# Splitting the last output projection of an attention + FFN kernel into early partial sums

## The chip, the cores and the metric

The kernel runs on one core of one Trainium2 chip. The metric is device time in microseconds (us) of one execution; lower is better. A span is the part of it that the profile shows, some 2 us shorter. Every run also lists its mean granted TensorE clock (1.0 is full speed). All runs quoted here are of the state "fast", the undisturbed one. In the views of the profile PE is TensorE, PEld its weight loads, DVE is VectorE, ACT ScalarE, POOL GpSimd and SP SyncE, which here only starts transfers; Lnnn is a line of the kernel.

## The reference

One transformer layer in parallel form: `x + attention(layernorm(x)) + ffn(layernorm(x))`, with 2048 tokens, width 640, 32 query heads of 20 channels that share one K and one V head, and a hidden layer of 1536 with squared ReLU. Data is bf16.

```python
# cut to what matters
q = (xn @ wq).reshape(B, S, 32, 20); k = xn @ wk; v = xn @ wv
p = softmax(q k^T * 20 ** -0.5)
attn = (p @ v).reshape(B, S, 640) @ wo      # the output projection
h = relu(xn @ w1 + b1) ** 2
out = x + attn + h @ w2 + b2
```

## The kernel before

Attention is done in 32 blocks: 4 chunks of 512 queries, and in each chunk 8 groups of 4 heads. A block has 16 steps of 128 keys, so there are 512 steps. In each step TensorE computes scores into PSUM banks 0 to 5, ScalarE exponentiates them (two instructions of 128x1024), and TensorE multiplies the result by V into bank 6 (the PV matmuls). Everything else (Q projection, FFN, normalisation, output projection) is cut into small pieces that a planner puts under the exponentials, one after the other through the one remaining bank, MISCB (7). Where a step has room, padding matmuls on zeros keep TensorE busy.

At the end of a block the accumulator is copied, transposed, divided by the softmax sum and transposed back into `OTn[:, chunk, group]`. The output projection of a chunk needs all 8 groups, so that of the last chunk can only start when every exponential is done:

```python
def op_pe(tt, ch, part=None):            # 128 tokens tt, half ch of the 640 columns
    gs = list(range(G)) if part is None else ...   # 8 head groups, in two parts of 4
    pairs = [(OTn[:, qc % 2, g, tl * 128:(tl + 1) * 128],
              wo_pad[:, g, ch * WOC:(ch + 1) * WOC]) for g in gs]
    ... mm_group(e, bank(MISCB, WOC), pairs, first, last)

def op_evac(tt, ch):                     # out_stage = PSUM + out_acc (fp32: x + FFN)
    ... e.tensor_tensor(out=out_stage[...], in0=bank(MISCB, WOC), in1=out_acc[...], op=ALU.add)

# [cut] the main loop over 512 steps, then:
pe_pv(NU - 1, 0)
fin_done_slot[NB - 1] = chain_fin(NB - 1, NU)      # last block's normalise/transpose
for tt in range(4 * (QC - 1), 4 * QC):             # the last chunk's 4 x 2 pieces
    for ch in range(2):
        op_pending.append((tt, ch, fin_done_slot[NB - 1] + 1))
```

## Time and profile before

| | before |
|---|---|
| time, median of the first 4 runs | 1014.39 us (1011.52 to 1017.11) |
| the profiled run | 1011.52 us, span 1009.8 us |
| ScalarE busy | 965.1 us, 96% of the span |
| last PV matmuls start | 988.95 us |
| the 8 projection pieces of the tail | 992.80 to 1007.51 us |

From the page of the profiled run of the kernel before: its span and the busy time of each engine.

```profile
span 1009.8 us, 16754 instructions
PE 821.8 (81%) x7425; PEld 297.7 (29%) x7483; DVE 212.5 (21%) x429; ACT 965.1 (96%) x1070; POOL 101.5 (10%) x138
```

ScalarE (ACT) sets the pace. The waits view says how much of its time the 1024 exponentials lost; columns are engine and line, what it waited for, total us, times, longest.

```profile
ACT PT L1092 <- PE ps L1076: 10.5, 12, 6.7
```

Only 10.5 us in the whole span, so work that lies under the exponentials is free as long as it does not hold them up. What is not free is the end. The chain of waits that ended last, in order of time (start, length, what), kernel before:

```profile
988.95 0.43 PE ps L1104 x4
...
992.32 0.43 DVE OTn L1169
992.75 0.05 issue
992.80 1.27 PE ps L462 x8
994.08 0.02 issue
994.10 0.50 DVE out_stage L1256
994.60 0.05 issue
994.65 1.27 PE ps L462 x8
...
1007.02 0.49 DVE out_stage L1256
```

TensorE multiplies 8 head groups (1.27 us), VectorE adds (0.50 us), TensorE waits for the bank and starts the next piece; the two steps from engine to engine, called hops here, take 0.02 and 0.05 us. That makes 1.84 us a round, eight rounds, 14.71 us. No engine is busy for more than part of it. Then the last store takes 2.3 us to the end of the span.

### The profile page before, as it was taken

The page shows a single profiled execution, that of the slowest core. Times are in us where ns is not written, and L with a number is a line of the kernel's source. Part 1 is how long each engine was busy: PE and PEld are TensorE (multiplying, and loading weights), DVE is VectorE, ACT ScalarE, POOL GpSimd, SP SyncE. Part 2 cuts the span into 40 slices and gives each one's busy share as a digit, 9 for nine tenths or more (in the row PEclk, how much of TensorE's full clock was granted, in tenths as well). Part 3 has the DMA queues.
Part 4 walks back from the last instruction along what each step waited for, and adds up shares of the span by engine and source line. Part 5 has one row for each costly group of instructions (what it writes and reads, how often), then busy time and mean ns, then how long its engine had stood idle before and what let it go on. Part 6 is the DMA issues. An engine that isn't in the chain of part 4 may idle for free.

```text
span 1009.8 us, 16754 instructions
## 1 busy us (share of the span) xinstructions
PE 821.8 (81%) x7425; PEld 297.7 (29%) x7483; DVE 212.5 (21%) x429; ACT 965.1 (96%) x1070; POOL 101.5 (10%) x138
## 2 busy tenths in 40 slices
PE   2878899878988887899888889987778877777775
PEld 2322244222432322244222224432222222222222
DVE  6522222222222222222222122210111111011102
ACT  6599999999999999999999999999999999999991
POOL 7021100121000012100120020000000000000000
PEclk9999999999999999999999999999999999999999
DMA  9100000000000000000000000000000000000000
GB/s 303 26 1 1 1 1 2 1 2 1 2 1 14 14 1 2 1 1 1 1 2 14 14 1 2 1 1 1 1 1 8 14 8 1 1 1 1 1 1 26
DMA packets 9433, 11.93 MB, mean 12 GB/s; under 512 B 1809, under 2 KB 8722, under 8 KB 9362
## 3 DMA queue, kind: packets, MB, share of 16 engines
q1 hardware_dynamic: 9362, 10.87, 3.3%
q8 instruction: 58, 0.95, 0.4%
q14 instruction: 13, 0.11, 0.0%
HBM read 8.25 MB, written 2.62 MB: 11 GB/s over the span
## 4 chain that ended last, share of the span: by engine, by line
ACT 89%; PE 7%; DVE 3%; issue 0%; DMA 0%; ACTq 0%; POOL 0%; SPq 0%; DVEq 0%
ACT PT L1092 88%; PE ps L462 2%; PE ps L1108 1%; PE ps L1076 1%; PE ps L1104 1%; DVE O_un L1135 1%; PE ps L1142 1%; ACT PT L632 1%; DVE out_stage L1256 1%; DVE r_tmp L908 1%; PE ps L722 0%; ACT PT L637 0%; PE ps L996 0%; DMA x_sb<-in_A_x_dram 0%; DVE xnT L737 0%
## 5 line engine op out<-in xcount | busy, mean ns | idle before, releaser
L1092 ACT ACTIVATE PT<-ps 128x1024 bf16<-128x1024 f32 x1024 | 940.1, 1237 | 10.5 <-PE ps L1076 10.5
L1076 PE MATMUL ps<-QT,KT_aug 21*128 21x512 bf16 x2048 | 202.4, 385 | 126.5 <-ACT PT L1092 121.0
L1108 PE MATMUL ps<-ones_bf,zeros_bf 128*32 128x512 bf16 x883 | 261.7, 380 | 0.0
L1104 PE MATMUL ps<-PT,V_aug 128*32 128x512 bf16 x2048 | 205.1, 390 | 8.0 <-DVE O_un L1135 7.3
L1076 PEld LDWEIGHTS ps<-QT,KT_aug 21*128 21x128 bf16 x2048 | 51.9, 91 | 320.9 <-ACT PT L1092 300.8
L1108 PEld LDWEIGHTS ps<-ones_bf,zeros_bf 128*32 128x32 bf16 x883 | 85.1, 96 | 53.9 <-issue 0.3
L954 POOL TENSOR_TENSOR Qsq<-QT 128x512 bf16<-128x512 bf16 x32 | 33.2, 1038 | 656.3 <-DVE QT L949 646.5
L1104 PEld LDWEIGHTS ps<-PT,V_aug 128*32 128x32 bf16 x2048 | 52.5, 93 | 125.5 <-issue 108.7
L462 PE MATMUL ps<-xnT,w_sb 128*128 128x512 bf16 x216 | 64.6, 383 | 4.2 <-issue 2.4
L915 POOL TENSOR_TENSOR h2T<-r_tmp 128x512 bf16<-128x512 bf16 x48 | 49.9, 1039 | 177.2 <-DVE r_tmp L908 177.2
L908 DVE TENSOR_SCALAR r_tmp<-ps,b_sb 128x512 bf16<-128x512 f32 x48 | 36.0, 751 | 136.1 <-PE ps L462 136.1
L462 PE MATMUL ps<-w_sb,h2T 128*128 128x160 bf16 x768 | 64.2, 233 | 0.0
L1135 DVE COPY O_un<-ps 128x512 f32<-128x512 f32 x32 | 22.0, 688 | 183.4 <-PE ps L1108 162.2
L462 PEld LDWEIGHTS ps<-w_sb,h2T 128*128 128x128 bf16 x768 | 51.6, 98 | 27.2 <-DVE out_acc L1216 21.7
L933 PE MATMUL ps<-xnT,wq_raw 128*20 128x512 bf16 x640 | 52.1, 382 | 8.0 <-issue 8.0
L462 PE MATMUL ps<-wo_pad,OTn 128*128 128x320 bf16 x256 | 44.5, 301 | 4.6 <-DVE out_stage L1256 4.1
L1216 DVE TENSOR_TENSOR out_acc<-ps,x_sb 128x160 f32<-128x160 f32 x64 | 20.8, 325 | 103.3 <-PE ps L462 103.3
L949 DVE CAST QT<-ps 128x512 bf16<-128x512 f32 x31 | 21.4, 692 | 99.7 <-PE ps L933 99.7
L963 DVE SCALAR_TENSOR_TENSOR QT<-ps,sc,QT 128x512 bf16<-128x512 f32 x32 | 24.0, 751 | 49.8 <-PE ps L958 49.7
L1256 DVE TENSOR_TENSOR out_stage<-ps,out_acc 128x320 bf16<-128x320 f32 x32 | 15.7, 492 | 83.9 <-PE ps L462 83.9
L462 PEld LDWEIGHTS ps<-wo_pad,OTn 128*128 128x128 bf16 x256 | 20.5, 97 | 33.1 <-issue 18.3
L1169 DVE COPY OTn<-ps 128x512 bf16<-128x512 bf16 x32 | 13.6, 424 | 71.6 <-PE ps L1161 71.6
(109 smaller groups left out, 274.7 us busy)
## 6 DMA issues: line engine op xcount, KB each, us to landing
w_sb<-in_B_w_dram SPq DMA_DIRECT2D x2, 1920.0 KB, 13.5
x_sb<-in_A_x_dram SPq DMA_DIRECT2D x8, 320.0 KB, 5.4
out_dram<-out_stage SPq DMA_DIRECT2D x16, 160.0 KB, 1.8
wq_raw<-in_A_wq_dram SPq DMA_DIRECT2D x1, 800.0 KB, 7.3
wo_pad<-in_A_wo_dram SPq DMA_DIRECT2D x4, 200.0 KB
wk_raw<-in_A_wk_dram SPq DMA_DIRECT2D x1, 25.0 KB, 6.6
wv_raw<-in_A_wv_dram SPq DMA_DIRECT2D x1, 25.0 KB, 5.8
b_raw<-in_B_b_dram SPq DMA_DIRECT2D x1, 3.0 KB
```

The costliest lines, as they stand in the source:

```text
L462: ins = e.matmul(outap, lhsT=l, rhs=r, start=(first and i == 0), stop=(last and i == n - 1))
L908: pl.op("dve", (lambda e, j=j, b=b, s=s: e.tensor_scalar(out=r_tmp[:, s, :], in0=bank(b), scalar1=b1_sb[:, j:j + 1], scalar2=0.0, op0=ALU. ...
L915: pl.op("pool", (lambda e, j=j, c=c, s=s: e.tensor_tensor(out=h2T[:, c % 2, j, :], in0=r_tmp[:, s, :], in1=r_tmp[:, s, :], op=ALU.mult)), ...
L933: ins = e.matmul(ps[32 * r:32 * r + DH, b * 512:(b + 1) * 512], lhsT=wq_raw[:, ft, h * DH:(h + 1) * DH], rhs=xnT[:, ft, qc * 512:(qc + 1) ...
L954: pl.op("pool", (lambda e, s=s: e.tensor_tensor(out=Qsq[:], in0=QT[:, s, :], in1=QT[:, s, :], op=ALU.mult)), reads=[rQT[s]], writes=[rQSQ] ...
L963: pl.op("dve", (lambda e, s=s, b=b: e.scalar_tensor_tensor(out=QT[:, s, :], in0=bank(b), scalar=scc(C_CVEC), in1=QT[:, s, :], op0=ALU.add, ...
L1076: ins = e.matmul(bank(bk), lhsT=KT_aug[32 * r:32 * r + 21, kc * 128:(kc + 1) * 128], rhs=QT[32 * r:32 * r + 21, qs, :], start=True, stop=True,
L1092: pl.op("act", (lambda e, bk=bk, s=s: e.activation(out=PT[:, s, :], in_=ps[:, bk * 512:bk * 512 + 1024], func=ACT.Exp, scale=SCALE)), read ...
L1104: ins = e.matmul(ps[32 * c:32 * c + 32, ACCB * 512:ACCB * 512 + 512], lhsT=V_aug[:, kc, :], rhs=PT[:, s, (c % 2) * 512:(c % 2) * 512 + 512 ...
L1108: ins = e.matmul(ps[0:32, ACCB * 512:ACCB * 512 + 512], lhsT=zeros_bf[:, 0:32], rhs=ones_bf[:, 0:512], start=False, stop=True, tile_positi ...
L1135: pl.op("dve", lambda e: e.tensor_copy(out=O_un[:], in_=bank(ACCB)), reads=[rB[ACCB]], writes=[rOUN], expect={rB[ACCB]: ("acc", blk, KC - ...
L1256: pl.op("dve", (lambda e, tt=tt, ch=ch, ss=ss: e.tensor_tensor(out=out_stage[:, ss, ch * WOC:(ch + 1) * WOC], in0=bank(MISCB, WOC), in1=ou ...
```

## The change

For the last chunk, groups 0-3 and then 4-5 are multiplied as soon as they exist and added into the fp32 accumulator, under the exponentials of later blocks. After the last block only groups 6-7 remain: 2 matmuls per piece, over six banks (the scores need them no more). The stores become eight of half width on three queues. The diff, cut to its core:

```diff
+        OPP_STAGES = [list(range(0, 4)), list(range(4, G - 2))]
+        OPP_AFTER_G = [3, G - 3]
+        OPF_GS = list(range(G - 2, G))
+        def opp_evac(tt, ch, stage):          # out_acc = PSUM + out_acc
+            ... e.tensor_tensor(out=out_acc[...], in0=bank(MISCB, WOC), in1=out_acc[...], op=ALU.add)
+        tail_dma_q = ["sp", "act", "pool"]
+        def op_final(tt, ch, bnk, idx):
+            op_pe(tt, ch, gs=OPF_GS, bnk=bnk, first=True, last=True, tagname="opf")
+            ... e.tensor_tensor(out=stg, in0=bank(bnk, WOC), in1=out_acc[...], op=ALU.add)
+            ... e.dma_start(out2d[tt * 128:(tt + 1) * 128, ch * WOC:(ch + 1) * WOC], stg)
@@ planning of each block
+                if pqc == QC - 1 and pg in OPP_AFTER_G:
+                    ... op_pending.append((tt, ch, fin_done_slot[blk - 1] + 1, stage))
@@ tail
-        fin_done_slot[NB - 1] = chain_fin(NB - 1, NU)
-        ... the eight pieces through MISCB
+        fin_evac_acc(NB - 1); fin_fwdT(NB - 1); ... fin_evac(NB - 1)
+        tail_banks = [0, 1, 2, 3, 4, 5]
+        ... op_final(tt, ch, tail_banks[idx % len(tail_banks)], idx)
```

## The prediction

> **What bounds the kernel now.** ScalarE: the table of engines gives it 965.1 of 1009.8 us (96%). Its 1024 exponentials start every 0.917 us (the timeline shows 32 in 29.66 us); in steady state the chain of waits is that line alone, and the waits view charges them only 10.5 us of idleness, so nothing done beneath them gains much. What is left is the serial ends. In the chain by time the last PV matmuls follow at 988.95 us, then the normalise-and-transpose steps of the last head group (to 992.75), then eight rounds of [8 matmuls 1.27 us, DVE add 0.50, hops 0.02 and 0.05] = 1.84 us, serial because all share one PSUM bank. They take 992.80 to 1007.51, 14.7 us; the last store needs 2.3 us more.
>
> **What the change does.** For the last query chunk, head groups 0-3 and 4-5 are multiplied earlier and added into the fp32 accumulator, under the exponentials. Only groups 6-7 stay: 2 matmuls per tile half, spread over six banks. The stores become eight of half width, on three queues.
>
> *Removed from the tail:* eight rounds, 14.7 us.
> *Left there:* the first pair of matmuls, 1.27 - 6 x 0.137 = 0.45 us (estimate: eight took 1.26 us, mean 301 ns, so about 0.137 apart); then VectorE limits: a pair costs PE about 0.27 us, an add 0.49 (group of the old eviction), about 0.52 with its hop. 0.45 + 8 x 0.52 = 4.6 us. The last add ends near 997.4 instead of 1007.5: 10.1 us less.
> *Added under the exponentials:* 16 DVE adds of about 0.49 us = 7.9 us on an engine 21% busy; the projection's matmul count is unchanged, some padding matmuls go. From 811 us on DVE does 6 instructions per 29.3 us block, so the shared bank has room; I expect all 16 pieces placed before the exponentials end. Where an old projection piece fell on a block boundary (784 to 789 us), the exponentials lost about 0.34 us (accumulator copies 59.01 us apart over two blocks against 58.67). Three boundaries: up to 1 us back, expected 0.3.
> *Stores:* the last is on ScalarE's queue; I expect the same 2.3 us. Two go through GpSimd. The Trainium skill, "DMA: Bandwidth & Descriptors", Specifications, gives about 1 us to first byte there against 0.6 for the others; the before trace has no such store to check. The sixth tile half ends about 1 us before the last, so it should about tie: expected loss 0.1 us.
>
> **Sum.** 14.7 - 4.6 - 0.4 = 9.7 us saved, 1.0%, all on the critical path. Predicted 1004.6 us, range 1001 to 1008. Faster by over 2% (under 994.1 us) 0.01; within 2% 0.97; slower 0.02.
>
> **What shows it right or wrong.** Last PV matmuls near 989 us as before (later: the pieces disturbed the exponentials). In the timeline's tail eight adds about 0.52 us apart with PE ahead, starting at 993.3, ending near 997.4. Chain of waits: DVE adds in place of matmul/add alternation. Idleness before the exponentials still 10 to 11 us. Span near 1000.
>
> **What would make it wrong.** GpSimd's store ending 1 us or more after the others, or the added queues lengthening start or end outside the span; pieces stalling PE in order, so the exponentials lose microseconds; pieces left over after the exponentials; slower adds; TensorE's clock dropping with fewer paddings.

## The result, and the profile after

| | before | after |
|---|---|---|
| median | 1014.61 us (16 runs, 1011.43 to 1017.11) | 1002.06 us (11 runs, 1000.42 to 1007.15) |
| profiled run | 1011.52 us, span 1009.8 | 1002.03 us, span 1000.0 |
| last PV to last add (traces) | 988.95 to 1007.51: 18.56 us | 989.32 to 997.76: 8.44 us |

The ratio is 0.9884, 95% interval 0.9868 to 0.9899. Ratios here are the mean time of one kernel's fast runs over that of the other's of the same rounds, so not quite the ratio of the medians.

The page of the changed kernel, the same two lines, and the waits of its exponentials:

```profile
span 1000.0 us, 16724 instructions
PE 818.1 (82%) x7401; PEld 295.2 (30%) x7459; DVE 220.3 (22%) x445; ACT 965.0 (96%) x1070; POOL 103.0 (10%) x140
```

```profile
ACT PT L1093 <- PE ps L1077: 10.1, 11, 6.7
```

VectorE is busy 7.8 us more (16 adds of 0.49) and the exponentials did not wait longer. From the last exponential that had to wait (near 789 us in both) to the last PV matmuls both traces take 199.99 us, and all 16 early pieces lie in that stretch. All early pieces sit where they were meant to; from the timeline of VectorE, changed kernel (start, length, engine, line, operation, operands, idle time before):

```profile
887.36 0.49 DVE L1267 TENSOR_TENSOR out_acc<-ps,out_acc 128x320 f32<-128x320 f32 x1 [0.82 <-PE ps L463]
889.19 0.49 DVE L1267 TENSOR_TENSOR out_acc<-ps,out_acc 128x320 f32<-128x320 f32 x1 [1.34 <-PE ps L463]
...
```

The last of them starts at 958.80, long before the exponentials end. The tail, from the timeline of the changed kernel:

```profile
993.21 3.65 PE L463 MATMUL ps<-wo_pad,OTn 128*128 128x320 bf16 x16 [0.52 <-DVE OTn L1170]
993.96 3.80 DVE L1293 TENSOR_TENSOR h2T<-ps,out_acc 128x320 bf16<-128x320 f32 x8 [0.81 <-PE ps L463]
...
995.83 0.79 POOL L1298 DMA_DIRECT2D out_dram<-h2T  x1 [51.86 <-DVE h2T L1293]
997.28 0.56 POOL L1298 DMA_DIRECT2D out_dram<-h2T  x1 [0.66 <-DVE h2T L1293]
```

Matmuls and adds overlap, and the 14.71 us have become 4.55. The chain of waits of the changed kernel in this tail:

```profile
993.21 1.79 PE ps L463 x6
...
995.03 0.50 DVE h2T L1293
...
995.83 0.79 POOL out_dram L1298
```

In this run it goes through six matmuls, one add and GpSimd's store, not through the adds as predicted. But the sixteen matmuls take 3.65 us, 0.228 each, where the prediction had 0.137. The windows view of TensorE in stretches of the tail shows why; columns are stretch, its length, busy us (instructions), granted clock, DMA share, GB/s. First the changed kernel, then the kernel before:

```profile
989.00:992.00 3.00, 1.05 (x8) 1.00 0.00 0
992.00:993.00 1.00, 0.44 (x4) 0.74 0.00 0
993.00:995.00 2.00, 1.79 (x7) 0.50 0.00 0
995.00:996.00 1.00, 1.00 (x5) 0.55 0.33 105
996.00:997.00 1.00, 0.86 (x7) 1.00 0.24 75
```

```profile
989.00:992.00 3.00, 1.12 (x10) 1.00 0.00 0
992.00:993.00 1.00, 0.48 (x6) 1.00 0.00 0
993.00:995.00 2.00, 1.41 (x11) 1.00 0.00 0
```

In the changed kernel's profiled run TensorE's clock was halved from about 992.5 to 995.9 us; in the run of before it was not, although TensorE had been about as idle (1.12 of 3 us) before the projection. The Trainium skill, "TensorE: Matmul & The Clock Gate", Part 1, describes this: an activity monitor halves the clock after at least one idle window of about 3.4 us, and the window runs freely, so that it depends on the run where it falls. The measured 3.4 us at 0.50 agree with its length. But TensorE was not idle in the 3.4 us before the drop: it was busy for 1.25 of them (windows view, 989.05 to 992.45).

So two things were to be explained. The two profiles differ by 9.8 us of span, almost exactly the predicted 9.7, while the medians differ by 12.55. And the predicted length of the new tail (4.6 us) was right although its clock was not.

### The profile page after: what moved, and what is told of

Same layout as the page of the kernel before. It is cut to its first block, busy times and chain, and to the rows that moved or that the text cites. A ratio compares the mean times of both kernels' runs of the same rounds, so it can differ in the third digit from the quotient of the medians.

```text
span 1000.0 us, 16724 instructions
## 1 busy us (share of the span) xinstructions
PE 818.1 (82%) x7401; PEld 295.2 (30%) x7459; DVE 220.3 (22%) x445; ACT 965.0 (96%) x1070; POOL 103.0 (10%) x140
## 4 chain that ended last, share of the span: by engine, by line
ACT 91%; PE 6%; DVE 2%; issue 0%; DMA 0%; POOL 0%; POOLq 0%; SPq 0%; DVEq 0%; ACTq 0%
ACT PT L1093 89%; PE ps L463 1%; PE ps L1109 1%; PE ps L1077 1%; PE ps L1105 1%; DVE O_un L1136 1%; PE ps L1143 1%; ACT PT L633 1%; DVE r_tmp L909 1%; PE ps L723 1%; ACT PT L638 0%; PE ps L997 0%; DMA x_sb<-in_A_x_dram 0%; DVE KT_aug L785 0%; DVE xnT L738 0%
## 5 line engine op out<-in xcount | busy, mean ns | idle before, releaser
L1093 ACT ACTIVATE PT<-ps 128x1024 bf16<-128x1024 f32 x1024 | 940.0, 1240 | 10.1 <-PE ps L1077 10.1
L1109 PE MATMUL ps<-ones_bf,zeros_bf 128*32 128x512 bf16 x859 | 255.9, 379 | 0.0
L1109 PEld LDWEIGHTS ps<-ones_bf,zeros_bf 128*32 128x32 bf16 x859 | 82.7, 96 | 50.9
L463 PE MATMUL ps<-wo_pad,OTn 128*128 128x320 bf16 x256 | 47.3, 308 | 0.5 <-DVE OTn L1170 0.5
L1307 DVE TENSOR_TENSOR out_stage<-ps,out_acc 128x320 bf16<-128x320 f32 x24 | 11.8, 492 | 73.0 <-PE ps L463 73.0
```

What stands on the lines that cost most here:

```text
L463: ins = e.matmul(outap, lhsT=l, rhs=r, start=(first and i == 0), stop=(last and i == n - 1))
L1093: pl.op("act", (lambda e, bk=bk, s=s: e.activation(out=PT[:, s, :], in_=ps[:, bk * 512:bk * 512 + 1024], func=ACT.Exp, scale=SCALE)), read ...
L1109: ins = e.matmul(ps[0:32, ACCB * 512:ACCB * 512 + 512], lhsT=zeros_bf[:, 0:32], rhs=ones_bf[:, 0:512], start=False, stop=True, tile_positi ...
```

## The experiments

**Theory.** The kernel's work is as predicted, and the rest is TensorE's clock: it halves for some windows in the tail and elsewhere, in some runs and not in others. The profile of before was a lucky run. **Rivals:** the difference of medians is start-up jitter; the early pieces alone or the extra banks alone do the work; GpSimd's stores set the end.

### 1 and 2: keep TensorE busy before the tail

Nine dummy matmuls go into TensorE's waits around the last transposes, in the kernel before (x1) and in the changed one (x2). The edit shown is x2's; x1 hands the same three groups to the planner's slots after the last step, and its trace shows them as 3 and 6.

```diff
+        def keep_warm(n):   # n matmuls of 128x512 into bank 2
         fin_evac_acc(NB - 1)
+        keep_warm(3)
         fin_fwdT(NB - 1)
+        keep_warm(4)
         fin_recip(NB - 1); fin_mult(NB - 1); fin_backT(NB - 1)
+        keep_warm(2)
         fin_evac(NB - 1)
```

> The kernel before, with 9 dummy matmuls of 128x512 put into TensorE's waits between the last PV matmuls and the tail projection (3, 4 and 2), so that TensorE is not idle there. Theory (clock): most runs of before meet a halved TensorE clock in the tail, and its profiled run happened not to. Then this kernel runs at about 1011.5 us in nearly every round, 3 us below the median of before, its tail matmuls take 1.27 us per eight in every profile, and the two groups of times of before (near 1011.5 and near 1015.5) shrink to one. Rival (prologue or launch jitter makes the two groups): the times stay spread between 1011 and 1017, median near 1014.6. Second rival (dummies only cost): up to 0.3 us slower.

> The changed kernel with the same 9 dummy matmuls. Clock theory: the first pair of tail matmuls takes 0.45 us in place of 0.73, the 16 matmuls of the tail 2.4 us in place of 3.65; VectorE's eight adds stay at about 0.475 us each and still set the length, so only 0.3 to 0.5 us of span is won: about 1001.6 us. If TensorE's clock mattered for the whole tail of the changed kernel, 1.2 us would be won.

x2: 1000.82 us median (1000.38 to 1001.04), span of its profile 998.4. The timeline of its tail:

```profile
992.42 2.35 PE L463 MATMUL ps<-wo_pad,OTn 128*128 128x320 bf16 x16
992.91 3.27 DVE L1293 TENSOR_TENSOR h2T<-ps,out_acc 128x320 bf16<-128x320 f32 x8 [0.54 <-PE ps L463]
```

At full clock the sixteen matmuls take 2.35 us, as the clock theory said. But the eight adds now take 3.27 us, 0.40 from start to start (3.27 less one add of 0.49, over seven), not the 0.475 that I had expected to stay. In the profiled run of the changed kernel VectorE had been fed too slowly. So the clock cost more than the 0.3 to 0.5 us that I had expected: 0.83 us from last PV to last add (8.44 in the changed kernel's trace, 7.61 in x2's). The medians differ by 1.2 us, but they come from different rounds. That the dummies kept the clock up is not shown by this one trace, because x5 below has a full clock in its tail without them; for them speaks that two of x2's four runs have a mean clock of 1.0 and none of the changed kernel's twelve has. This also shows the prediction's second error, hidden by the first: an add takes 0.49 us by itself but the next one starts 0.40 us after it, so the tail at full clock is 0.49 (first pair of matmuls and hop) + 3.27 (eight adds) = 3.76 us, not 4.6.

x1: 1012.83 us median (1010.79 to 1015.25); ratio 0.9991, 0.9967 to 1.0015: no change that could be told from noise. My expectation was a miss. Its profiled run was a slow one (span 1013.4) with a full clock and the usual 1.84 us rounds in the tail, so its loss lies elsewhere. The windows view by 2.5 us finds it; columns are stretch, length, busy us of PE, PEld, DVE, ACT and POOL (instructions), clock, DMA share, GB/s. First the kernel before, then x1:

```profile
110.00:112.50 2.50, 2.34 (x24) 0.75 (x23) 0.95 (x2) 2.12 (x4) 0.00 (x0) 1.00 0.00 0
```

```profile
110.00:112.50 2.50, 2.50 (x11) 0.98 (x9) 0.26 (x1) 0.87 (x1) 0.00 (x0) 0.50 0.00 0
```

And the exponentials in ScalarE's timeline: the first of the main loop and the first of this block, in the kernel before and then in x1 (the number in brackets is the wait before it):

```profile
44.96 7.44 ACT L1092 ACTIVATE PT<-ps 128x1024 bf16<-128x1024 f32 x8 [6.68 <-PE ps L1076]
110.65 117.48 ACT L1092 ACTIVATE PT<-ps 128x1024 bf16<-128x1024 f32 x128 [0.39 <-PE ps L1076]
```

```profile
46.11 34.94 ACT L1092 ACTIVATE PT<-ps 128x1024 bf16<-128x1024 f32 x38 [6.68 <-PE ps L1076]
112.78 117.48 ACT L1092 ACTIVATE PT<-ps 128x1024 bf16<-128x1024 f32 x128 [1.91 <-PE ps L1076]
```

ScalarE waits 0.38 or 0.39 us at this block boundary in every other trace. In x1 the clock halved there (and again near 230 us), and it waited 1.91 us instead (1.86 at the second). So the clock also drops in the main loop, at 1.5 us each time here, and the dummies in the tail can't help that. The traces of x4, x5, x9 and x12 have one such drop each, at 1.4 to 1.5 us. The profiled run of before had one too, near 49 us, which cost it only 0.54 us.

The rival "start-up jitter" is true in part. The main loop of x1 began 1.15 us later than that of before (46.11 against 44.96 us), of 3.6 us of difference in span; over the 13 traces it begins between 44.51 and 46.11 us.

The mean clock of each run sorts the kernel before. Its 29 runs in the three later sets of rounds:

| mean clock of the run | runs | time, us |
|---|---|---|
| 0.998 | 12 | 1010.98 to 1013.21 |
| 0.995 to 0.997 | 8 | 1013.32 to 1015.50 |
| 0.991 to 0.993 | 9 | 1015.50 to 1016.95 |

The profiled run of before was one of the best class. The clock alone does not set the time: that class is two groups, six runs from 1010.98 to 1011.54 us and six from 1012.87 to 1013.21, so it must matter where the clock is lost, or something else differs. None of x1's six runs was below 0.997. That fits a slow class which comes from the tail, but six runs are few.

### 3 and 4: banks alone, early pieces alone

x3 keeps all 8 groups in the tail but spreads the pieces over six banks (`OPP_AFTER_G = []`, `OPF_GS = range(G)`). x4 keeps the early pieces but puts the tail back into one bank:

```diff
-        tail_banks = [0, 1, 2, 3, 4, 5]
+        tail_banks = [MISCB]
```

> The changed kernel without the early pieces: all 8 head groups stay in the tail (64 matmuls), but over six banks and with the new stores. Estimate at full clock: 64 x 0.137 + 0.3 = 9.1 us of matmuls, then one add: last add 9.6 us after the start of the projection against 14.7 before and 4.6 changed. If the clock is halved for its first 3 us, 1.5 us more. So about 5 us of the gain come from the banks alone: 1007 to 1008 us. Theory 'the early pieces do it, banks are incidental' expects this near 1013.

> The changed kernel with all eight tail pieces in one PSUM bank again: early pieces without the overlap. Estimate at full clock: eight rounds of 0.45 + 0.50 + 0.07 = 1.02 us = 8.2 us, at half clock throughout 1.3 us each = 10.4 us, against 3.8 + 0.75 measured for the changed kernel: 1006 to 1008 us. TensorE would be busy only a third of the time, so I expect the clock to stay halved, near 1008. If the gains of pieces and banks simply added up, this would be at 1014.6 - 12.5 + (gain of x3).

x3: 1007.94 us (ratio 0.9941), x4: 1007.52 us (0.9939), against 1013.21 for before in the same rounds, both as expected. Each half alone is worth about 5.5 us (5.3 and 5.7), so neither is incidental. x4 lies where I expected it at half clock; TensorE's timeline of x4 shows rounds going from full to half clock:

```profile
994.22 0.45 PE L463 MATMUL ps<-wo_pad,OTn 128*128 128x320 bf16 x2 [0.52 <-DVE OTn L1170]
995.25 0.71 PE L463 MATMUL ps<-wo_pad,OTn 128*128 128x320 bf16 x2 [0.58 <-DVE h2T L1293]
996.54 0.71 PE L463 MATMUL ps<-wo_pad,OTn 128*128 128x320 bf16 x2 [0.59 <-DVE h2T L1293]
```

The two matmuls of a piece take 0.45 us at first and 0.71 afterwards, and stay at 0.71 to the end: in this serial tail TensorE is busy for 0.71 of each 1.30 us, and the clock does not come back.

### 12 and 13: the same two with dummies

> Banks alone (no early pieces, 64 matmuls in the tail over six banks) with the 9 dummy matmuls, so at full clock. 64 x 0.137 + 0.3 = 9.1 us plus one add of 0.49: the first of eight groups after 1.27 us, then one per 1.09 us. About 1.4 us below the kernel without dummies (1007.9): 1006.5 us.

> Early pieces alone (all tail pieces in one bank) with the 9 dummy matmuls. Two matmuls 0.45, add 0.50, hops 0.07: 1.02 us per round in place of the 1.30 seen at half clock, as long as the clock holds; TensorE is busy only 0.3 to 0.45 us of each round, so the clock should halve again at the next chance, after 3 to 7 us: 1006 to 1007 us, against 1007.5 without dummies.

x12: 1006.58 us, as expected; x13: 1005.73 us (1005.22 to 1009.69), a little under the expected 1006 to 1007. In x12 the two runs with clock 1.0 took 1005.46 and 1005.66, the two with 0.998 took 1007.5 and 1007.6; the profile, one of the latter, has a clock drop in the main loop near 375 us and a clean tail. TensorE of x12's tail, then of x13's:

```profile
994.11 8.87 PE L463 MATMUL ps<-wo_pad,OTn 128*128 128x320 bf16 x64
```

```profile
996.49 0.45 PE L463 MATMUL ps<-wo_pad,OTn 128*128 128x320 bf16 x2 [0.59 <-DVE h2T L1293]
998.60 0.71 PE L463 MATMUL ps<-wo_pad,OTn 128*128 128x320 bf16 x2 [0.59 <-DVE h2T L1293]
```

From the first matmul to the last add: before 14.71 us, banks alone 9.39 (994.11 to 1003.50), pieces alone 8.78 (992.36 to 1001.14), both 3.76 (x2). The two gains, 5.3 and 5.9, nearly add up to the 10.95 of both. x13 kept the full clock for six rounds and lost it in the seventh, 6 us after the last dummy, as expected; so its 8.78 us contain two rounds at half clock.

### 9 and 10: a halved clock on purpose

The padding matmuls of the last 3 of 512 steps are dropped, in before (x9) and after (x10):

```diff
-            npad = sl.npad(u)
+            npad = sl.npad(u) if u < NU - 3 else 0
```

> The kernel before without padding matmuls in the last 3 of its 512 steps, to bring TensorE's halved clock into the tail on purpose. Theory: half clock from about 989 to 992 us in every run; while it lasts, eight matmuls take about 2.3 us in place of 1.27, a round 2.9 in place of 1.84; with TensorE then busy 78% of the time it returns to full speed after some rounds or never: between 2 and 8 us slower than a clean run of before (1011.2), so 1013 to 1019, and the fastest run above 1012.5. Rival (the tail's clock plays no part in the spread): same spread and same fastest run as before, 1011.

> The changed kernel without padding matmuls in the last 3 steps. It has only 16 matmuls in the tail instead of 64, and VectorE hides part of them, so a halved clock costs it little: at half clock throughout 16 x 0.267 + 0.3 + 0.5 = 5.1 us from first matmul to last add, against 3.8 with full clock and 4.55 in its profiled run. 1002 to 1003 us, in every run within 1.5 us of the changed kernel, where the same edit costs the kernel before 2 to 8 us.

x9: 1016.05 us, all six runs between 1014.97 and 1018.09 with clocks of 0.990 to 0.993. The fastest run is 4 us above the fastest of before (1010.98), so a half clock in the tail removes the fast runs; that it makes the slow class of before is not shown, because no slow run of before has a trace. Against the mean of before the ratio is 1.0019, 0.9999 to 1.0039, no difference clear of noise. The timeline of x9's tail:

```profile
995.30 2.31 PE L462 MATMUL ps<-wo_pad,OTn 128*128 128x320 bf16 x8 [0.52 <-DVE OTn L1169]
998.20 2.11 PE L462 MATMUL ps<-wo_pad,OTn 128*128 128x320 bf16 x8 [0.59 <-DVE out_stage L1256]
1000.90 1.26 PE L462 MATMUL ps<-wo_pad,OTn 128*128 128x320 bf16 x8 [0.59 <-DVE out_stage L1256]
```

Two rounds at half clock cost 1.9 us, the transposes before them 0.9 more (4.73 us from last PV to projection against 3.85). Here a drop in the main loop near 522 us adds 1.4 us; the profile does not reach the 7 us of the slowest runs.

x10: 1002.51 us (1001.91 to 1002.74), as expected. In its profile the last PV to the last add took 9.71 us against 7.61 in x2, so a tail halved from end to end costs the changed kernel 2.1 us. That is not much less than the 2.8 us in x9's profile: a shorter tail is less exposed, but this pair does not show by how much.

### 5: no store through GpSimd

```diff
-        tail_dma_q = ["sp", "act", "pool"]
+        tail_dma_q = ["sp", "act"]
```

> The changed kernel with its eight tail stores on two queues only (SP and ScalarE in turn, none through GpSimd). In the changed kernel's profile the chain of waits ends in GpSimd's second store, but ScalarE's last store was issued 0.5 us later and lands at about the same time. If GpSimd's stores set the end, the span falls by up to 0.5 us; if they only tie, nothing: 1001.7 to 1002.1 us. More than 0.5 us would mean that GpSimd's queue costs something else.

x5: 1001.76 us (1001.50 to 1001.78), ratio 0.9875 to before, against 0.9884 for the changed kernel in other rounds: a tie. But the two profiles, both of 1000.0 us, are not alike: x5's lost 1.4 us to a clock drop near 375 us and then had a full clock in its tail, without dummies:

```profile
994.18 2.35 PE L463 MATMUL ps<-wo_pad,OTn 128*128 128x320 bf16 x16 [0.52 <-DVE OTn L1170]
994.66 3.27 DVE L1293 TENSOR_TENSOR h2T<-ps,out_acc 128x320 bf16<-128x320 f32 x8 [0.54 <-PE ps L463]
```

These are x2's 2.35 and 3.27 us again; TensorE's work before them was that of the changed kernel (1.25 of 3.4 us). What the stores cost is read from the end: the last add ends at 997.93 and the span at 1000.0, 2.07 us later, against 2.24 in the changed kernel and 2.22 in x2. GpSimd costs at most some 0.2 us there. Outside the span (time less span) x5's runs have a median of 1.76 us, those of the changed kernel 1.97, so its queue may cost another 0.2. Its store took a median of 2.1 us from issue to landing, those of SP and ScalarE 1.6, for 80 KB; the 1 and 0.6 us to first byte that the prediction takes from the Trainium skill, "DMA: Bandwidth & Descriptors", Specifications, are in keeping.

### 7 and 11: a version that beats both

The experiments say that after the last head group the time goes to VectorE's adds, and that TensorE should stay busy before them. x7 gives four of the eight evictions to ScalarE, which is idle there, multiplies group 6 in TensorE's waits, and adds the accumulator of ScalarE's four pieces by an fp32 identity matmul, which also keeps TensorE busy. Stores are four of full width.

```diff
+        # before the last transposes: bank = out_acc (fp32 identity matmul, ScalarE's pieces) + group 6
+        pre(0, 0); pre(1, 0)
         pe_pv(NU - 1, 0)
+        fin_evac_acc; pre(2, 0); fin_fwdT; ...; pre(3, 0); pre(0, 1); pre(1, 1); fin_backT; pre(2, 1); fin_evac
+        # after them: one matmul (group 7) per piece; the eighth piece still has two
+        ScalarE: e.activation(out=stg, in_=bank(...), func=ACT.Copy)          # half 0 of each tile
+        VectorE: e.tensor_tensor(out=stg, in0=bank(...), in1=out_acc, op=add)  # half 1
```

> A version meant to beat both kernels. On top of the changed kernel: head group 6 is multiplied before the last transposes, in TensorE's waits (which also keeps it busy), so one matmul per tile half is left after the last head group; ScalarE, idle in the tail, evicts four of the eight halves (for these the accumulator is added by an fp32 identity matmul beforehand), VectorE the other four; four full-width stores on SP. If eviction sets the tail (theory), the length from the last transposed group to the last eviction falls from 3.8 us (kernel with dummies) or 4.55 (changed) to about 0.4 + 4 x 0.42 = 2.1 us: about 999 us, span near 996.5. If TensorE's clock were all that mattered, it would equal the kernel with dummies, 1000.8.

x7: 999.80 us, ratio 0.9860: 1.0 us below x2 in the medians, but of other rounds, and the intervals of the ratios overlap; less was won than expected. TensorE's timeline shows what went wrong; the last exponential had ended at 988.12 (timeline of ScalarE):

```profile
987.58 0.81 PE L1474 MATMUL ps<-out_acc,ident_f 128*128 128x320 f32 x2
988.22 0.30 PE L1478 MATMUL ps<-wo_pad,OTn 128*128 128x320 bf16 x1
988.36 0.70 PE L1474 MATMUL ps<-out_acc,ident_f 128*128 128x320 f32 x2
988.89 0.30 PE L1478 MATMUL ps<-wo_pad,OTn 128*128 128x320 bf16 x1
989.12 0.40 PE L1105 MATMUL ps<-PT,V_aug 128*32 128x512 bf16 x4
```

In the trace TensorE takes them in the program's order. The last PV matmuls, which the whole tail waits for, stood behind the second fp32 identity matmul and started 1.0 us after that exponential, against 0.05 in the kernel before. x11 moves that work behind them:

```diff
-        pre(0, 0); pre(1, 0)
+        piece(0, 0, [G - 2], ident=True)               # only one ahead of the PV; that step's padding dropped
         pe_pv(NU - 1, 0)
+        piece(1, 0, [], ident=True); ...                # the rest in later waits
-        all four stores on SP
+        the fourth store on ScalarE's queue
```

> The split-eviction version mended: in its profile the last PV matmuls began 1.0 us after the last exponential had ended, held up by two fp32 identity matmuls queued ahead of them. Now only one stands ahead (and the padding of that step is dropped), the others fill later waits, and the last store goes out on ScalarE's queue. Expected: last PV within 0.1 us of the last exponential again, last eviction 2.2 us after the last transposed group, store 2.2 us: 0.8 to 1.2 us below the first version's clean runs (999.5), so about 998.5 us. If the delay was not from the identity matmuls, no gain.

x11: 999.16 us (998.86 to 999.26), ratio 0.9856 to before. The timeline of its tail:

```profile
988.46 0.40 PE L1105 MATMUL ps<-PT,V_aug 128*32 128x512 bf16 x4 [0.30 <-ACT PT L1093]
...
992.65 1.66 ACT L1507 ACTIVATE h2T<-ps 128x320 bf16<-128x320 f32 x4 [4.25 <-PE ps L1478]
992.79 1.85 DVE L1510 TENSOR_TENSOR h2T<-ps,out_acc 128x320 bf16<-128x320 f32 x4 [0.54 <-PE ps L1478]
```

The PV matmuls start 0.06 us after the last exponential (988.40) again, and the last eviction ends at 994.64, 6.18 us after the PV started, against 7.61 in x2 and 8.44 in the changed kernel's profile. It is 0.6 us faster than x7 in the medians, somewhat less than the 0.8 expected, and 2.9 us faster than the changed kernel, none of whose runs was under 1000.42. The medians come from different rounds; against before of the same rounds the ratios are 0.9856 and 0.9884.

## Why the prediction was right or wrong

The range (1001 to 1008, around 1004.6) held the measured 1002.06, and "within 2%" was right. Point by point:

- *ScalarE bounds the kernel; only the tail is to be won.* Right: its busy time stayed at 965 us, the gain lies between the last PV and the last add, 18.56 to 8.44 us, which is 10.1 us less, the figure predicted. That the spans too differ by 9.8 us, near the predicted 9.7, is partly luck: the 0.4 us allowed for losses did not occur (the early pieces cost nothing that shows, and the end after the last add is 2.24 us against 2.29), but the changed kernel's main loop began 0.91 us later (45.87 against 44.96), of which the kernel before lost 0.54 to its drop near 49 us.
- *Early pieces are free.* Right, and better than the 0.3 us allowed: the waits after 789 us are the same in both traces. That the exponentials waited 10.1 us in all against 10.5 is not owed to them: the difference is one wait of 0.43 us of before at 52.8 us, at its drop of the clock, in code that both kernels share.
- *The tail is 0.45 + 8 x 0.52 = 4.6 us.* The measured 4.55 is right by two errors that cancel. The step "about 0.52 with its hop" was mis-sized: fed in time, adds start 0.40 us apart (x2), so the next one starts before the profiled 0.49 us of the last are over. And "PE ahead" failed in the profiled run: half clock made the first pair 0.75 us with its hop and the feeding slow; the chain of waits goes through the matmuls. The hop belongs to the serial chain of before, not to a stream.
- *GpSimd's stores about tie.* Right to some 0.2 us of span (x5), where 0.1 was allowed.
- *"TensorE's clock dropping with fewer paddings"* was listed as a risk, but for the wrong reason. The padding lies elsewhere; the drop followed the idle stretch around the last transposes, which the kernel before has as well (busy 1.27 of 3.4 us); before and x5 kept the full clock through it, so whether it comes is a matter of the run.
- *9.7 us off a median of 1014.39.* This step failed by 2.5 us. I took the saving from one profile and subtracted it from the median, without seeing that the profiled run (1011.52) was nearly the fastest of its kernel and had a full clock in its tail. From the profiled run, 1011.52 - 9.7 = 1001.8, the measured 1002.06 would have been met. The changed kernel's profile stands at its median (1002.03 against 1002.06), that of before 3.1 us below its own. The sorted table ties the slow runs of before to a lower clock, but no run shows what removes them: x1, made to, did not move the median clearly.

What stays open is what the slow runs of before lose, since none of them has a trace, and so where the 2.5 us come from. Drops in the main loop are seen (x1, x4, x5, x9, x12) at about 1.5 us, half clock in the tail can be made (x9, 2.8 us), the start of the main loop shifts by up to 1.6 us, and x1 had none of the slow class in six runs (before: 9 of 29). Nor is it known why ten of the changed kernel's twelve runs, the profiled one included, agree within 0.7 us (1001.6 to 1002.3, with one at 1000.42 and one at 1007.15), while before spreads over six: the code of the first 870 us is the same.

## What to carry to other kernels

In the tail of a kernel count the rounds of a shared PSUM bank: each one pays matmul, eviction and hops in series, and early partial sums and more banks cut different parts of that sum (5.9 and 5.3 us here, 10.95 together), so both were worth doing. Before subtracting a saving found in one profile from a median, check that the profiled run stands near the median, and compare the granted clock in the stretch that matters in both. Work put into TensorE's waits should stand behind, not ahead of, the matmul that the critical path needs next: x7 lost 1.0 us that way.

## What the Trainium skill lacked or had wrong

- "TensorE: Matmul & The Clock Gate" names an idle window (Part 1), and its closing table of rules tells the reader to avoid idle gaps above about 3 us. Here the clock halved in the changed kernel with no idle gap above 1.1 us, after 3.4 us of which TensorE was busy for 1.25, and near 109 us of x1 with no gap above 0.7 us, after 3.4 us of which it was busy for 2.04. Part 1 also tells of a kernel whose frequent short idles made the clock swing, but gives no busy share at which it is lost, and that is what a kernel writer needs. The runs do not give one either: the same stretches in before (1.27 and 2.04 of 3.4 us) and in x5 (1.25) kept the full clock, which agrees with the page's free-running window.
- The same page says that about 3.4 us of sustained work bring the clock back, but not what share of busy time counts as that. With rounds busy 0.71 of 1.30 us (x4) it stayed at 0.50 to the end, some 9 us; with rounds of 2.3 in 2.9 and 2.1 in 2.7 us (x9) it returned after two, and after 2.88 busy of 3.4 us in the changed kernel.
- "Perfetto Trace Analysis", Optimizing Scalar/DVE Operations, says that the profiled time of an instruction contains an acknowledgement that overlaps the next instruction. This case agrees and gives a size: adds of 128x320 from PSUM profiled at 0.49 us ran 0.40 us apart (x2, x5), so costing a stream by profiled lengths was 0.09 us per add too much. "VectorE: DVE Perf Modes", The DRAIN you can't avoid, says that the next operation does not start until the pipe is empty, and then that one which is not held starts earlier; no run here separates the two.
